# A state-space layer and a mixer MLP on one core: the spectrum of the second chunk taken once, kernel sums a step sooner, part of x loaded by GpSimd

## The chip, the core and the metric

The kernel runs on one core of a Trainium2 chip, as one program. The core has TensorE (PE, with its weight loads as PEld), VectorE (DVE), ScalarE (ACT), GpSimd (POOL) and SyncE (SP), which issues most of the transfers between device memory and the core's own memory. The metric is device time of one execution in microseconds (us), as the median of several runs. One execution was also recorded by the hardware profiler; all rows below come from it.

## The reference

```python
def reference(u, log_A_real, A_imag, C_real, C_imag, log_dt, D_skip, w1, b1, w2, b2, c, w_mod):
    sa, ca, ga, sb, cb, gb = split(silu(c) @ w_mod, 6)        # each [448]
    h = layernorm(u) * (1 + ca) + sa                          # u: [2048, 448]
    # S4D: kernel K[d, l] = 2 Re sum_n C[d,n] exp(A[d,n] dt[d] l), 256 modes, 2048 taps
    y = irfft(rfft(h.T, 4096) * rfft(K, 4096))[:, :2048].T + h * D_skip
    x = u + ga * y
    h = layernorm(x) * (1 + cb) + sb
    # token-mixing MLP over the 2048 rows, 1792 hidden units, shared by the 448 columns
    h = layernorm(h)
    return x + gb * (gelu(h.T @ w1 + b1) @ w2 + b2).T
```

## The kernel before

**Steps.** The taps of K come from exponentials and sines, made in 56 steps of 8 columns (`NHALF`). A step is written as: `st_phase` (TensorE, L608: phases `xe`, `xg` from `lph` and `tab`, for the step after), `st_step` (ScalarE: six activations L649 to L654 on the phases; VectorE: the four products `E`; GpSimd: the two products `G`), and `st_kgen` (TensorE, L683: 32 small products of `G` and `E` into `kg`; after each second step ScalarE copies `kg` to `ks`, L697). `st_kgen` of step s stood in the code of step s + 2. The steps go in seven batches of 8; each opens with a `window`, in which ScalarE takes the 16 exponentials (L619) of the batch and TensorE the exponents, and in which the last two `st_kgen` of the batch before stand. `st_s1` (L721) transforms finished taps into `yk`.

**The Fourier product in pieces.** The columns of K are handled in two chunks of 224; a chunk has 16 pieces. For a piece n:

- `pc_load` (SyncE): `u`, a part of the spectrum of h that was written to memory as `us_d` earlier (L744 in the second chunk, L747 in the first), and tables `si` (L750, L752);
- `pc_s2` (TensorE, L780): `kx`, the spectrum of K, a table times `yk`;
- `pc_mul` (VectorE, L788): two products `z` of `kx` and `u`;
- `pc_inv` (TensorE, L796 and L797): `vv`, the inverse of the two `z`;
- `pc_out` (ScalarE, L802, then SyncE): copy to `vt` and write to `v_d`.

An fp32 matmul makes two records in the profile. The first chunk's pieces are put between the steps from step 33 on by `piece`: on odd steps a new piece's `pc_s2`, on even ones its `pc_inv`. The second chunk runs alone after the steps, in a loop over k (L1133), with loads three pieces ahead. Its order on TensorE is kx of the next piece, then vv of this one. In the second chunk `kx` was made twice, once by a table with the real part in both halves of the partitions and once by that table with its halves exchanged and a sign (`pc_swap` for the first piece, `pc_tables` for the others, tile `sw`, L761, L768, L769). GpSimd made the third table of a piece from the second (L770, L771). Each of the two was multiplied by the same `u`.

**Start.** x has 2048 rows, held as 16 rows `r` for each of 128 partitions (`xt`). Rows 0 to 3 are loaded by GpSimd, rows 4 to 15 by SyncE (`x_load`, L299, four transfers a call), ahead of the loads that the steps ask for: `lph` and `lex` (L594, L598: parameters) and blocks of w_mod (L324, `wm`, 784 KB each, by the table `late`: blocks 2 and 3 in steps 2 and 3). `u_stats` (L499) takes the statistics of rows 2s and 2s + 1 in step s, on VectorE in the middle of `st_step`. `modulation` (L486) multiplies a block of w_mod with the condition; block 2 is first asked for at the end of step 4.

**Order.** TensorE, ScalarE, VectorE and GpSimd run in the order in which the code is written. SyncE does so up to step 8 and near the end of the second chunk, and in between a scheduler sets its order. Every engine works its queue in order: whatever stands behind a waiting instruction waits too. After the second chunk the layer norms and the two MLP products follow (L1181 to L1183, L1304 to L1306).

Of the kernel before, what the change touches and what calls it, by code (L numbers as in the profile page):

```python
# [11 lines left out]
F32 = mybir.dt.float32  # L12
# [10 lines left out]
P = 128  # L23
# [16 lines left out]
def dft_tables():  # L40
    n1 = np.arange(32)
    k1 = np.arange(32)
    n2 = np.arange(64)
    k2 = np.arange(64)
    nn = 4096
    t = {}
    w = 2 * np.pi * np.outer(n1, k1) / 64
    w1 = np.zeros((2, 32, 32))
    w1[0] = np.cos(w)
    w1[1] = -np.sin(w)  # L50
    w1[0, :, 0] = 1
# [12 lines left out]
    def inverse(rows, cols, k, m, ang):  # L64
        a = np.cos(ang) * 2 / nn
        b = np.sin(ang) * 2 / nn
        i1[0, rows, k, m[0]] = a
        i1[1, rows, k, m[0]] = -b
        i2[1, rows, k, m[0]] = -a
        i2[0, rows, k, m[0]] = -b  # L70
        if len(m) > 1:
            i1[0, rows, k, m[1]] = b
            i1[1, rows, k, m[1]] = a
            i2[1, rows, k, m[1]] = -b
            i2[0, rows, k, m[1]] = a

    for k in range(1, 32):
        ang = 2 * np.pi * np.outer(n2, k + 64 * k2) / nn
        s[0, :, k, 0] = np.cos(ang)
        s[1, :, k, 0] = np.sin(ang)  # L80
        s[0, :, k, 1] = -np.sin(ang)
        s[1, :, k, 1] = np.cos(ang)
        inverse(slice(None), None, k, (0, 1), ang.T)


    for q in range(32):
        ang = 2 * np.pi * n2 * (32 + 64 * q) / nn
        s[1, :, 0, 0, q] = np.cos(ang)
        s[1, :, 0, 1, q] = -np.sin(ang)
        inverse(q, None, 0, (1,), ang)  # L90
    for q in range(33, 64):
        ang = 2 * np.pi * n2 * (64 * (q - 32)) / nn
        s[0, :, 0, 0, q] = np.cos(ang)
        s[0, :, 0, 1, q] = -np.sin(ang)
        inverse(q, None, 0, (0,), ang)
    s[0, :, 0, 0, 32] = 1
    s[0, :, 0, 1, 32] = (-1.0) ** n2
    i1[0, 32, 0, 0] = 1 / nn
    i2[1, 32, 0, 0] = (-1.0) ** n2 / nn
    s2 = s.reshape(P, 32 * P)  # L100

    t["S2"] = s.reshape(2, 4, 8, 2, 32 * P).transpose(3, 0, 2, 1, 4).reshape(P, 32 * P)

    one = np.einsum("cnk,cqkm->km", w1, s.reshape(2, 64, 32, P))
    t["SV"] = one[ones_k1()].T

    order = lambda a: a.reshape(P, 32, 2, 2, 2, 16).swapaxes(3, 4)
    t["I1"] = order(i1)
    t["I2"] = order(i2)
    ft = np.zeros((32, 2, 2, 32, 2))  # L110
    w = 2 * np.pi * np.outer(k1, n1) / 64
    f0 = np.cos(w)
    f1 = -np.sin(w)
    f0[0] = 1
    f1[0] = (-1.0) ** n1
    for h in range(2):
        ft[:, 0, h, :, h] = f0
        ft[:, 1, h, :, h] = f1
    t["FT"] = ft.reshape(P, 64)


    te = np.zeros((3, 64, 16, 32))
    tg = np.zeros((3, 16, 4, 16, 32))
    n = np.arange(32)
    for d in range(16):
        te[0, 2 * d : 2 * d + 2, d] = 2 * n + 1
        te[2, 2 * d : 2 * d + 2, d] = -n
        tg[0, d, 0:2, d] = n
        tg[0, d, 2:4, d] = 1
        tg[2, d, 0:2, d] = -64 * n  # L130
        tg[2, d, 2:4, d] = 1
    tg = tg.reshape(3, 16, 2, 2, 512).swapaxes(1, 2)
    tt = np.concatenate([te.reshape(3, 64, 512), tg.reshape(3, 64, 512)], 1)
    tt[1] = -tt[0]
    t["TT"] = tt.reshape(3, P, 512)

    v1, v2 = (t.pop(k).reshape(2, 64, 32, P) for k in ("I1", "I2"))
    j1 = np.stack([v1[0], v2[1]])  # L140
    j2 = np.stack([v1[1], v2[0]])
    for nm, tabs, n in (("SI", (s2, v1, v2), NP), ("SJ", (s2, j1, j2), 1)):
        t[nm] = np.stack([a.reshape(P, NP, 2, P)[:, :n] for a in tabs], 2).reshape(P, n * 6 * P)

    re = np.stack([s[:, :, :, 0]] * 2, 3)
    t["SK"] = np.stack([a.reshape(P, NP, 2, P) for a in (re, v1)], 2).reshape(P, NP * 4 * P)
    return {k: np.ascontiguousarray(v.astype(np.float32)) for k, v in t.items()}


# [72 lines left out]
def tile_adaln_s4d_mixer(ctx, tc, i, out):  # L224
# [20 lines left out]
    with ExitStack() as es:  # L245
# [49 lines left out]

        def x_load(r0, n, eng=nc.sync):
            for g in range(4):
                rr = slice(r0, r0 + n)
                eng.dma_start(xt[32 * g : 32 * g + 32, rr], xv[rr, g].rearrange("r n d -> n r d"))  # L299


        mg = cg.tile([P, 2, P], BF16, name="mg")
# [301 lines left out]
        def halves(out, lhs, rhs, start, stop):  # L604

            for k in range(2):
                r = slice(64 * k, 64 * k + 64)
                T.matmul(out[k], lhs[r], rhs[r], start=start, stop=stop)  # L608
# [147 lines left out]

        def pc_swap(n):

            pw[n] = swp.tile([P, 2, P], F32, tag="sw", name="sw")
            halves = lambda t: t.rearrange("p j (h m) -> p j h m", h=2)  # L760
            S.copy(halves(pw[n]), halves(pl[n][1][:, 0])[:, :, ::-1])  # L761

        def pc_tables(n):


            re, to, back = (pl[n][1][:, t] for t in range(3))
            pw[n] = im = swp.tile([P, 2, P], F32, tag="sw", name="sw")
            S.activation(im[0:64], re[64:128], AF.Copy, scale=-1.0)  # L768
            S.copy(im[64:128], re[0:64])  # L769
            G.tensor_copy(back[0:64], to[64:128])  # L770
            G.tensor_scalar(back[64:128], to[0:64], -1.0, None, ALU.mult)  # L771

        def pc_s2(n):
            c, p = divmod(n, NP)
            k1 = yks[c][:, 2 * p : 2 * p + 2]
            pk[n] = [(pxs if c else pms).tile([P, 2, DC], F32, tag="ms", name="kx") for _ in range(c + 1)]
            tabs = [pl[n][1][:, 0]] + ([pw.pop(n)] if c else [])
            for j in range(2):
                for kx, t in zip(pk[n], tabs):
                    T.matmul(kx[:, j], t[:, j], k1[:, j], start=True, stop=True)  # L780

        def pc_mul(n):
            c, p = divmod(n, NP)
            u = pl[n][0]
            pz[n] = []
            for cc in range(2):
                z = fp.tile([P, 2, DC], F32, tag=f"z{cc}", name=f"z{cc}")
                V.tensor_tensor(z, pk[n][cc if c else 0], u[:, 0 if c else cc], ALU.mult)  # L788
                pz[n].append(z)
            pk.pop(n)  # L790

# [124 lines left out]
        for g in (1, 2):  # L916
            load(g, False)
        wm_load(1, wm_slot(1))
        x_load(4, 4)
        x_load(8, 8)  # L920
        remainder()

        def chains():
# [43 lines left out]
        def window(s):  # L967
# [12 lines left out]
            for e in range(BATCH):  # L980
# [15 lines left out]
                if s == 8 and e == 1:  # L996

                    tt(mod[0], mod[0], mod[2], ALU.mult)
                if e < 2 and s:
                    st_kgen(s - 2 + e)  # L1000
                elif e == 5:
                    if s == 8:
                        yks[0] = y0.tile([P, 32, DC], F32, tag="yk", name="yk0")
                    st_s1(s > 16)
# [28 lines left out]
        for s in range(tail):  # L1033
# [30 lines left out]
            if s >= NHALF:  # L1064
                flush(dve)
                mellow()
            else:
                if s % BATCH > 1:
                    st_kgen(s - 2)
                if (s + 1) % BATCH:  # L1070
                    st_phase(s + 1)
                elif s + 1 < NHALF:
                    st_exponents(s + 1)
                st_step(s, between)
            flush(act)
            if s == NHALF:
                st_kgen(s - 2)
                st_kgen(s - 1)

            free = s > 7 and not st_s1(s % BATCH == BATCH - 1)  # L1080
            if s + 2 < 32 and (s + 2) % BATCH > 1:
                st_mag2(s + 2)
# [50 lines left out]
        for k in range(NP + 1):  # L1133

            n = NP + k
            if k < NP:
                if n + 3 < 2 * NP:
                    pc_load(n + 3)
                pc_s2(n)
                pc_mul(n)  # L1140
            if k + 1 < NP:
                pc_tables(n + 1)
            if k:
                pc_inv(n - 1)
                pc_out(n - 1)
            if k == NP - 4:
                last = ExitStack()
                last.enter_context(tc.manual_schedule(engines={ENG.SP}))

            if k in (NP - 3, NP - 2):  # L1150
                wst.load()
                if k == NP - 3:
                    x_pair(0)
# [184 lines left out]
```

## Time and profile before

| what | us |
|---|---|
| median of 3 runs | 752.48 |
| their lowest and highest | 751.7, 760.46 |
| the profiled execution: its time | 759.6 |
| its span, first to last instruction | 757.8 |

| stretch of the profiled execution | us from the span's start |
|---|---|
| steps 0 to 31 | 27 to 253 |
| steps 32 to 55, with the first chunk's pieces | 253 to 386 |
| second chunk | 399 to 449 |
| layer norms and MLP | 449 to 758 |

A row of a timeline is: start, duration, engine, line, operation, out<-in with shapes and count, and in brackets the idle time of the engine just before it and what ended it. A row of groups is: line, engine, operation, names, shapes and count, then busy us in total, mean ns of one, and idle time before with its releasers. A row of windows is: stretch, its length, busy us of PE, PEld, DVE, ACT and POOL with counts, granted TensorE clock (1.00 is full), DMA share (mean busy share of the 16 DMA engines) and GB/s.

### The profile page before, as it was taken

How to read it: one execution, taken by the hardware profiler on the slowest of the kernel's cores; microseconds unless marked ns; L12 is line 12 of the kernel's file. 1: busy time of each engine (PE TensorE's matmuls, PEld its weight loads, DVE VectorE, ACT ScalarE, POOL GpSimd, SP SyncE). 2: the span in 40 equal slices, each digit the busy share in tenths (PEclk: the TensorE clock that was granted, in tenths of full speed). 3: DMA queues.
4: the chain of work that ended last, by engine and by line, in shares of the span. 5: the costliest groups of instructions: out<-in, count | busy, mean ns of one | idle time of the engine just before them, and what ended most of it. 6: DMA issues, size and time to landing. Idle time of an engine off the chain costs nothing. (4 is left out here: it accounts for less than half of the span.)

```text
span 757.8 us, 18128 instructions
## 1 busy us (share of the span) xinstructions
PE 667.6 (88%) x7136; PEld 497.6 (66%) x7136; DVE 453.4 (60%) x875; ACT 448.3 (59%) x842; POOL 249.4 (33%) x289
## 2 busy tenths in 40 slices
PE   1779989969789878888889966999999999999997
PEld 0435334535435556556579963777899999999996
DVE  7695878599478568584863335677752253433341
ACT  5956587788687788988944445777742242222220
POOL 6573456438337766766733310000000000000000
PEclk9878657969899889999999995999999999999999
DMA  6884545286777736545456789985566426566540
GB/s 166 235 175 116 172 142 176 74 251 172 206 188 240 201 87 166 141 129 151 114 161 205 238 229 264 224 217 160 141 190 207 144 68 189 154 173 181 148 134 25
DMA packets 97106, 127.99 MB, mean 169 GB/s; under 512 B 12922, under 2 KB 78206, under 8 KB 96894
## 3 DMA queue, kind: packets, MB, share of 16 engines
q1 hardware_dynamic: 96398, 125.14, 59.4%
q0 software_dynamic: 624, 1.70, 0.8%
q8 instruction: 56, 0.92, 0.5%
q14 instruction: 28, 0.23, 0.1%
HBM read 91.46 MB, written 34.87 MB: 167 GB/s over the span
## 5 line engine op out<-in xcount | busy, mean ns | idle before, releaser
L209 ACT CAST whi<-w 128x896 fp32r<-128x896 f32 x64 | 59.8, 939 | 131.4 <-PE o L1305 84.7
L656 POOL TENSOR_TENSOR G<-mag,gs 128x512 f32<-128x512 f32 x56 | 71.8, 1282 | 119.0 <-ACT gs L652 118.9
L218 DVE TENSOR_TENSOR wlo<-w,whi 128x896 fp32r<-128x896 f32 x64 | 67.9, 1086 | 40.3 <-ACT whi L209 27.9
L1181 PE MATMUL acc<-h3h,whi 128*128 128x448 f32 x224 | 83.6, 373 | 0.0
L1182 PE MATMUL acc<-h3l,whi 128*128 128x448 f32 x224 | 82.2, 367 | 0.0
L608 PE MATMUL xg<-tab,lph 64*128 64x512 f32 x112 | 68.6, 615 | 15.1 <-ACT xg L654 8.4
L683 PEld LDWEIGHTS kg<-E,G 128*32 128x32 f32 x3584 | 61.2, 122 | 31.0 <-issue 15.9
L1183 PE MATMUL acc<-h3h,wlo 128*128 128x448 f32 x224 | 81.4, 364 | 0.0
L1305 PE MATMUL o<-ul,whi 128*128 128x448 f32 x224 | 81.3, 363 | 0.0
L1304 PE MATMUL o<-uh,whi 128*128 128x448 f32 x224 | 81.2, 362 | 0.0
L1306 PE MATMUL o<-uh,wlo 128*128 128x448 f32 x224 | 80.6, 360 | 0.0
L608 PE MATMUL xe<-tab,lph 64*128 64x512 f32 x112 | 66.6, 602 | 11.1 <-ACT gs L653 9.3
L683 PE MATMUL kg<-E,G 128*32 128x64 f32 x3584 | 71.4, 239 | 5.3 <-issue 4.9
L657 POOL TENSOR_TENSOR G<-mag,gs 128x512 f32<-128x512 f32 x56 | 71.9, 1284 | 0.0
L658 DVE TENSOR_TENSOR E<-m,xe 128x512 f32<-128x512 f32 x56 | 38.1, 681 | 49.2 <-ACT xe L651 23.6
L637 POOL TENSOR_TENSOR m<-mag,w 128x512 f32<-128x512 f32 x56 | 59.8, 1068 | 5.6 <-DVE E L662 1.2
L788 DVE TENSOR_TENSOR z<-kx,u 128x448 f32<-128x448 f32 x64 | 36.8, 616 | 41.1 <-PE kx L780 41.1
L1308 DVE SCALAR_TENSOR_TENSOR y<-o,b,mod 128x448 f32<-128x448 f32 x16 | 10.9, 684 | 80.3 <-PE o L1306 80.3
L649 ACT ACTIVATE ab<-xe 128x512 f32<-128x512 f32 x56 | 33.5, 599 | 33.0 <-PE xe L608 18.7
L1181 PEld LDWEIGHTS acc<-h3h,whi 128*128 128x128 f32 x224 | 42.7, 191 | 13.0 <-ACT h L1236 7.8
L608 PE MATMUL xe<-tab,lex 64*128 64x512 f32 x56 | 31.8, 584 | 16.5 <-DMA lex<-wm 15.9
L619 ACT ACTIVATE mag<-xe 128x512 f32<-128x512 f32 x56 | 34.2, 611 | 18.9 <-PE xg L608 10.6
(222 smaller groups left out, 1545.2 us busy)
## 6 DMA issues: line engine op xcount, KB each, us to landing
w<-in_B_w_dram SPq DMA_DIRECT2D x64, 224.0 KB
w<-in_B_w_dram SPq DMA_DIRECT2D x32, 448.0 KB
u<-us_d SPq DMA_DIRECT2D x48, 224.0 KB
yu_d<-yt SPq DMA_DIRECT2D x16, 448.0 KB
yi<-yu_d SPq DMA_DIRECT2D x16, 448.0 KB
us_d<-uo SPq DMA_DIRECT2D x16, 448.0 KB
v_d<-vt SPq DMA_DIRECT2D x32, 224.0 KB
vt<-v_d SPq DMA_DIRECT2D x16, 448.0 KB
```

What stands on the lines that cost most here:

```text
L209: self.nc.scalar.copy(hi, w)
L218: eng.tensor_tensor(lo, w, hi.bitcast(F32), ALU.subtract)
L608: T.matmul(out[k], lhs[r], rhs[r], start=start, stop=stop)
L656: G.tensor_tensor(Gt[:, 1], mg_, v32(sg), ALU.mult)
L657: G.tensor_tensor(Gt[:, 0], mg_, v32(cg_), ALU.mult)
L683: T.matmul(kgs[g][32 * q : 32 * q + 32, m], Gt[:, c, d], E[:, c, d], start=h == 0 and c == 0 and m == 0, stop=h == 1 and c == 1, skip_grou ...
L1181: nc.tensor.matmul(acc[f], hi[:, fs], h3h[:, r], start=r == 0, stop=False)
L1182: nc.tensor.matmul(acc[f], hi[:, fs], h3l[:, r], start=False, stop=False)
L1183: nc.tensor.matmul(acc[f], lo[:, fs], h3h[:, r], start=False, stop=r == 15)
L1304: nc.tensor.matmul(o, hi[:, ks], uh[kh][:, k], start=kh == 0 and k == 0, stop=False)
L1305: nc.tensor.matmul(o, hi[:, ks], ul[kh][:, k], start=False, stop=False)
L1306: nc.tensor.matmul(o, lo[:, ks], uh[kh][:, k], start=False, stop=kh == 1 and k == 6)
```

## The change

Three edits.

1. In the second chunk `kx` is made once, by the table `s2` that the first chunk has too (real part in one half of the partitions, imaginary part in the other). The first `z` is `kx` times `u`, the second `kx` times `u` with its halves exchanged. `pc_swap` now copies `u` (two copies of 64 partitions by 448 columns, by ScalarE) for every piece, a piece ahead, and `pc_tables` has three GpSimd instructions where it had two, and none on ScalarE. The memory table `SK` holds `s2` and `v1`, as large as before.
2. From step 33 on, `st_kgen` of step s stands in the code of step s + 1, behind the phase.
3. Rows 4 to 7 of x are loaded by GpSimd behind its work of step 0, rows 8 to 15 behind that of step 1, in transfers of the same sizes.

```diff
+    for nm, tabs, n in (("SI", (s2, v1, v2), NP), ("SJ", (s2, j1, j2), 1), ("SK", (s2, v1), NP)):
...
         def pc_swap(n):
-            pw[n] = swp.tile([P, 2, P], F32, tag="sw", name="sw")
-            halves = lambda t: t.rearrange("p j (h m) -> p j h m", h=2)
-            S.copy(halves(pw[n]), halves(pl[n][1][:, 0])[:, :, ::-1])
+            pw[n] = swp.tile([P, 2, DC], F32, tag="sw", name="sw")
+            for h in range(2):
+                S.copy(pw[n][64 * h : 64 * h + 64], pl[n][0][64 - 64 * h : 128 - 64 * h, 0])
 
         def pc_tables(n):
-            re, to, back = (pl[n][1][:, t] for t in range(3))
-            pw[n] = im = swp.tile([P, 2, P], F32, tag="sw", name="sw")
-            S.activation(im[0:64], re[64:128], AF.Copy, scale=-1.0)
-            S.copy(im[64:128], re[0:64])
-            G.tensor_copy(back[0:64], to[64:128])
-            G.tensor_scalar(back[64:128], to[0:64], -1.0, None, ALU.mult)
+            like, unlike = pl[n][1][:, 1], pl[n][1][:, 2]
+            G.tensor_copy(unlike[0:64], like[64:128])
+            G.tensor_copy(unlike[64:128], like[64:128])
+            G.tensor_scalar(like[64:128], like[0:64], -1.0, None, ALU.mult)
 
         def pc_s2(n):
-            pk[n] = [(pxs if c else pms).tile([P, 2, DC], F32, tag="ms", name="kx") for _ in range(c + 1)]
-            tabs = [pl[n][1][:, 0]] + ([pw.pop(n)] if c else [])
+            pk[n] = (pxs if c else pms).tile([P, 2, DC], F32, tag="ms", name="kx")
             for j in range(2):
-                for kx, t in zip(pk[n], tabs):
-                    T.matmul(kx[:, j], t[:, j], k1[:, j], start=True, stop=True)
+                T.matmul(pk[n][:, j], pl[n][1][:, 0, j], k1[:, j], start=True, stop=True)
 
         def pc_mul(n):
-                V.tensor_tensor(z, pk[n][cc if c else 0], u[:, 0 if c else cc], ALU.mult)
+                V.tensor_tensor(z, pk[n], pw.pop(n) if c and cc else u[:, cc], ALU.mult)
...
         first_chain()
-        x_load(4, 4)
-        x_load(8, 8)
...
         def window(s):
-                if e < 2 and s:
-                    st_kgen(s - 2 + e)
+                if s and e < (2 if s <= 32 else 1):
+                    st_kgen(s - (2 if s <= 32 else 1) + e)
...
-                if s % BATCH > 1:
+                if s < 32 and s % BATCH > 1:
                     st_kgen(s - 2)
                 if (s + 1) % BATCH:
                     st_phase(s + 1)
                 elif s + 1 < NHALF:
                     st_exponents(s + 1)
+                if s > 32 and s % BATCH:
+                    st_kgen(s - 1)
                 st_step(s, between)
             flush(act)
             if s == NHALF:
-                st_kgen(s - 2)
                 st_kgen(s - 1)
+            if s < 2:
+                x_load(4 + 4 * s, 4 + 4 * s, G)
...
             if k + 1 < NP:
                 pc_tables(n + 1)
+                pc_swap(n + 1)
```

Line numbers of the changed kernel are lower by 4 to 8 from the tables on (L683 is L679 there, L780 is L772, L796 and L797 are L788 and L789, L299 is L295).

**TensorE, steps 36 and 37.** The end of the phase of one step, a sum `kg`, the inverse `vv` of a piece and the beginning of the next phase. Before:

```order
L608 MATMUL xe<-tab,lph_142 128x512
L608 MATMUL xg<-tab,lph_142 128x512
L796 MATMUL vv<-z_3982,si 128x224
L797 MATMUL vv<-z_3984,si 128x224
L796 MATMUL vv<-z_3982,si 128x224
L797 MATMUL vv<-z_3984,si 128x224
L683 MATMUL kg<-E,G 32x64 x32
L608 MATMUL xe<-tab,lph_143 128x512
L608 MATMUL xg<-tab,lph_143 128x512
```

And in the changed kernel:

```order
L604 MATMUL xe<-tab,lph_142 128x512
L604 MATMUL xg<-tab,lph_142 128x512
L679 MATMUL kg<-E,G 32x64 x32
L788 MATMUL vv<-z_4014,si 128x224
L789 MATMUL vv<-z_4016,si 128x224
L788 MATMUL vv<-z_4014,si 128x224
L789 MATMUL vv<-z_4016,si 128x224
L604 MATMUL xe<-tab,lph_143 128x512
L604 MATMUL xg<-tab,lph_143 128x512
```

The sum has moved from behind vv to ahead of it, and it is that of a step later.

**ScalarE, beginning of the second chunk.** `yk` is the last transform of the taps, `sw` the swapped tile, `vt` the copy out. Before:

```order
L727 COPY yk_3487<-y_5856 128x32x2x8
L802 COPY vt<-vv 128x448
L761 COPY sw<-si 128x256
L768 ACTIVATE sw<-si 64x256
L769 COPY sw<-si 64x256
L768 ACTIVATE sw<-si 64x256
L769 COPY sw<-si 64x256
L802 COPY vt<-vv 128x448
```

And in the changed kernel:

```order
L723 COPY yk_3487<-y_5856 128x32x2x8
L794 COPY vt<-vv 128x448
L757 COPY sw<-u 64x448 x6
L794 COPY vt<-vv 128x448
L757 COPY sw<-u 64x448 x2
L794 COPY vt<-vv 128x448
```

Two copies of `u` a piece stand where two of the table stood, still ahead of the vt of two pieces earlier.

**SyncE and GpSimd, steps 0 to 4.** `wm_79` is w_mod, `lph` the parameters, `pars` their place in memory. SyncE before:

```order
L324 DMA wm_79<-in_w_mod_dram 112x4x448
L299 DMA xt<-in_A_u_dram 32x1792 x4
L299 DMA xt<-in_A_u_dram 32x3584 x4
L594 DMA lph_142<-pars_57 32x256
L598 DMA lph_142<-pars_57 64x1x256
L324 DMA wm_79<-in_w_mod_dram 112x4x448 x2
```

GpSimd in the changed kernel, from the products of step 0 on:

```order
L652 TENSOR_TENSOR G<-mag,gs 128x512
L653 TENSOR_TENSOR G<-mag,gs 128x512
L295 DMA xt<-in_A_u_dram 32x1792 x4
L631 TENSOR_TENSOR w<-mag 128x16
L633 TENSOR_TENSOR m_417<-mag,w 128x512
L652 TENSOR_TENSOR G<-mag,gs 128x512
L653 TENSOR_TENSOR G<-mag,gs 128x512
L295 DMA xt<-in_A_u_dram 32x3584 x4
```

The two L299 rows have left SyncE's queue, so that `lph_142` and the blocks of w_mod follow the first block directly, and stand in GpSimd's between the products of a step and the tables `m` of a later one.

More of the change, by code (lines that the diff above doesn't have):

```diff
@@ L141, in dft_tables @@
     j2 = np.stack([v1[1], v2[0]])
[L142 to L148, printed above, removed]
+    for nm, tabs, n in (("SI", (s2, v1, v2), NP), ("SJ", (s2, j1, j2), 1), ("SK", (s2, v1), NP)):
+        tabs = [a.reshape(P, NP, 2, P)[:, :n] for a in tabs]
+        t[nm] = np.stack(tabs, 2).reshape(P, n * len(tabs) * 2 * P)
     return {k: np.ascontiguousarray(v.astype(np.float32)) for k, v in t.items()}
@@ L297, in x_load @@
             for g in range(4):
-                rr = slice(r0, r0 + n)
-                eng.dma_start(xt[32 * g : 32 * g + 32, rr], xv[rr, g].rearrange("r n d -> n r d"))
+                to = xt[32 * g : 32 * g + 32, r0 : r0 + n].rearrange("n r d -> n (r d)")
+                eng.dma_start(to, x.rearrange("(n g r) d -> g n (r d)", g=4, r=16)[g, :, r0 * D : (r0 + n) * D])
         mg = cg.tile([P, 2, P], BF16, name="mg")
```

## Prediction

> **What bounds the kernel now.** I read the page first: shares, clock, and the chain that ended last.
>
> ```profile
> span 757.8 us, 18128 instructions
> PE 667.6 (88%) x7136; PEld 497.6 (66%) x7136; DVE 453.4 (60%) x875; ACT 448.3 (59%) x842; POOL 249.4 (33%) x289
> ...
> PEclk9878657969899889999999995999999999999999
> ...
> PE acc L1181 6%; PE acc L1182 6%; PE o L1305 6%; PE acc L1183 6%; PE o L1304 6%; PE o L1306 6%; PE kx L780 3%; PE y L1209 2%; PE vv L796 1%; PE vv L797 1%; DMA w<-in_B_w_dram 1%; DMA v_d<-vt 1%; SPq L1189 0%; SPq L1127 0%; ACT vt L802 0%
> ```
>
> TensorE leads; its granted clock is full (9) in the slices from 303 to 454 us. But half of this chain is the MLP (L1181 to L1306), which the change doesn't touch. What it touches is three stretches, each with a bound of its own, and no two of them overlap. So I price each and add.
>
> The second chunk (401 to 448 us) is TensorE alone. The chain in order of time shows it piece after piece:
>
> ```profile
> 425.87 1.51 PE kx L780 x8
> 427.38 0.38 PE vv L796 x2
> ...
> 428.52 0.38 PE vv L797 x2
> 428.89 1.51 PE kx L780 x8
> ```
>
> A piece takes 428.89 - 425.87 = 3.02 us, eight kx records and eight vv records of 0.189 us (1.51 / 8) with no wait between them.
>
> The kernel loop (steps 33 to 55) is a ring. Here is one pair of steps from the timeline, all engines, with the idle time and its releaser in brackets:
>
> ```profile
> 371.12 0.60 ACT L649 ACTIVATE ab<-xe 128x512 f32<-128x512 f32 x1 [0.76 <-PE xe L608]
> 374.25 0.60 ACT L649 ACTIVATE ab<-xe 128x512 f32<-128x512 f32 x1
> 374.50 1.14 DVE L788 TENSOR_TENSOR z<-kx,u 128x448 f32<-128x448 f32 x2
> 374.52 1.27 POOL L657 TENSOR_TENSOR G<-mag,gs 128x512 f32<-128x512 f32 x1
> 375.17 0.65 PE L796 MATMUL vv<-z,si 128*128 128x224 f32 x2 [1.06 <-DVE z L788]
> 377.03 1.10 PE L683 MATMUL kg<-E,G 128*32 128x64 f32 x64
> 377.25 0.55 ACT L802 COPY vt<-vv 128x448 f32<-128x448 f32 x1
> 378.06 0.50 PE L608 MATMUL xe<-tab,lph 64*128 64x512 f32 x1
> 378.20 0.37 ACT L697 COPY ks<-kg 128x256 f32<-128x256 f32 x1 [0.40 <-PE kg L683]
> 379.33 0.60 ACT L649 ACTIVATE ab<-xe 128x512 f32<-128x512 f32 x1 [0.76 <-PE xg L608]
> ```
>
> A pair lasts 379.33 - 371.12 = 8.21 us. ScalarE has two steps of 374.25 - 371.12 = 3.13 us, a vt copy and a ks copy in it, and stands idle for 0.40 + 0.76 us: it waits for kgen (377.03), and then for the phase (378.06) behind kgen. TensorE had itself been idle 1.06 us in front of vv.
>
> The start (28 to 62 us) waits for transfers. Rows of SyncE, VectorE, TensorE and GpSimd:
>
> ```profile
> 28.52 9.85 SPq L299 DMA_DIRECT2D xt<-in_A_u_dram  x8
> 40.95 1.27 SPq L324 DMA_DIRECT2D wm<-in_w_mod_dram  x2
> 41.91 0.63 DVE L499 BATCH_NORM_STATS2 st<-xt 128x6 f32<-128x448 f32 x1 [1.58 <-DMA xt<-in_A_u_dram]
> 57.24 3.35 PE L486 MATMUL pm<-wm,scb 112*128 112x448 f32 x4 [4.63 <-DMA wm<-in_w_mod_dram]
> ```
>
> Eight transfers of x hold SyncE's queue until 38.4, then come two blocks of w_mod, and TensorE stands from 52.61 to 57.24 for the first of them.
>
> **Part A, the spectrum once.** Each of the 16 pieces of the second chunk loses four of its eight kx records: 4 x 0.189 = 0.76 us, 16 x 0.76 = 12.1 us, if TensorE stays the bound. The first kx also loses a wait for the swapped table:
>
> ```profile
> 400.25 0.65 PE L780 MATMUL kx<-yk,sw 128*128 128x224 f32 x2 [0.59 <-ACT sw L761]
> ```
>
> That is 0.6 us. A piece is then 3.02 - 0.76 = 2.27 us. What is late next?
>
> ```profile
> L802 ACT COPY vt<-vv 128x448 f32<-128x448 f32 x32 | 17.3, 539 | 32.4 <-PE vv L797 19.8 <-issue 9.9 <-DMA v_d<-vt 1.8
> L788 DVE TENSOR_TENSOR z<-kx,u 128x448 f32<-128x448 f32 x64 | 36.8, 616 | 41.1 <-PE kx L780 41.1
> L769 ACT COPY sw<-si 64x256 f32<-64x256 f32 x15 | 6.0, 403 | 0.2
> L770 POOL COPY si<-si 64x256 f32<-64x256 f32 x15 | 5.9, 395 | 35.8 <-DMA si<-in_SK_dram 19.7 <-issue 8.0 <-PE vv L797 7.2
> L771 POOL TENSOR_SCALAR si<-si 64x256 f32<-64x256 f32 x15 | 12.7, 847 | 1.0
> ```
>
> ScalarE now swaps u in two copies of 64x448. Nothing of that shape stands in the trace: at least 0.40 each (L769, fewer columns), at most the 0.54 of L802 (same columns, from PSUM). I take 0.54, the same column count: 2 x 0.54 + 0.54 for vt = 1.6 us. VectorE stays at 2 x 0.62 = 1.2. GpSimd makes 0.40 + 0.40 + 0.85 = 1.65. All lie under 2.27, beside TensorE. ScalarE's swap of piece n+1 stands ahead of vt of n-1 and needs u a piece earlier than before. What lies queued behind it is vt, then the write of v_d, then SyncE's next u. The landing is judged from these rows:
>
> ```profile
> 438.04 0.33 SPq L752 DMA_DIRECT2D si<-in_SK_dram  x1
> 441.20 0.39 POOL L770 COPY si<-si 64x256 f32<-64x256 f32 x1 [1.01 <-DMA si<-in_SK_dram]
> ```
>
> Table 31 was in use 441.20 - 438.04 = 3.2 us after its issue. It is issued at the end of vv 27 and wanted by kx 31 two pieces later, 4.5 us at the new pace, so the buffers still reach. The traffic may not:
>
> ```profile
> 415.00:420.00 5.00, 5.00 (x28) 5.00 (x27) 2.25 (x4) 2.27 (x6) 2.48 (x4) 1.00 0.85 281
> 425.00:430.00 5.00, 5.00 (x28) 5.00 (x27) 1.32 (x3) 2.34 (x6) 1.68 (x4) 1.00 0.76 218
> ```
>
> The last two columns are DMA share and GB/s. A piece moves u, table and v_d, 224 + 256 + 224 KB = 0.721 MB. At full share these rows give 281 / 0.85 = 331 or 218 / 0.76 = 287 GB/s, so 2.18 to 2.51 us for a piece, on both sides of 2.27. I take the middle, 2.35, which costs 16 x 0.08 = 1.3 us. **A: 12.1 + 0.6 - 1.3 = 11.4 saved**; with 2.51 it is 8.9, with transfers that can't go faster than now it is 0.6, with no limit 12.7.
>
> **Part B, the sums a step sooner.** TensorE's order in a pair changes from vv, kgen, phase to kgen, vv, phase. The kgen (1.03 us, 377.03 to 378.06) goes into the 1.06 us in which TensorE waited for z. The phase then follows vv directly, about 377.0 to 378.2 with its L608 matmuls as long as before (378.06 to 379.33), and ScalarE has until 371.12 + 2 x 3.13 + 0.55 + 0.37 = 378.3 of its own work. So the pair becomes about 7.2 us, and its two waits, 1.16 us, all but go. Such brackets on ScalarE run from the row at 291.15 to that at 379.33:
>
> ```profile
> 291.15 0.60 ACT L649 ACTIVATE ab<-xe 128x512 f32<-128x512 f32 x1 [0.76 <-PE xe L608]
> ```
>
> Three pairs have both waits (1.16 or 1.17), two have 0.76 alone, two 0.41 alone: 5.8 us in all. In each of the two later windows of exponentials two kgens stood between the first exponents and now one does:
>
> ```profile
> 303.24 0.60 ACT L619 ACTIVATE mag<-xe 128x512 f32<-128x512 f32 x1 [1.06 <-PE xg L608]
> 347.60 0.60 ACT L619 ACTIVATE mag<-xe 128x512 f32<-128x512 f32 x1 [1.55 <-PE xg L608]
> 388.32 1.83 PEld L683 LDWEIGHTS kg<-E,G 128*32 128x32 f32 x128 [0.28 <-issue]
> ```
>
> One kgen less is 1.0 us in each, within both waits; and behind the last step (388.32) two kgens in a row become one, 1.0 more. Together 5.8 + 2.0 + 1.0 = 8.8. TensorE itself needs 8.21 - 1.06 = 7.15 us of a pair, so it is as full as ScalarE and small slips will show: **B: 8 saved**, between 3 and 9. The wait added is kgen for G of the step before. G of the step of 371.12 ended at 375.79 (374.52 + 1.27); its kgen is now asked for at 378.2. It is covered by 2.4 us. Queued behind a kgen that waited would be vv or kx and the next phase, and ScalarE behind that.
>
> **Part C, rows of x by GpSimd.** SyncE is free at 28.5 instead of 38.4 and issues the two blocks of w_mod some 10 us sooner, behind one reload of lph. GpSimd issues eight transfers instead:
>
> ```profile
> 7.66 2.00 POOL L299 DMA_DIRECT2D xt<-in_A_u_dram  x4
> 43.19 1.27 POOL L656 TENSOR_TENSOR G<-mag,gs 128x512 f32<-128x512 f32 x1 [1.46 <-ACT gs L652]
> 40.00:45.00 5.00, 5.00 (x28) 1.97 (x28) 3.35 (x7) 3.09 (x6) 3.46 (x5) 0.50 0.95 202
> ```
>
> Its own four took 0.5 us each; SyncE's took 9.85 / 8 = 1.23. I take 0.5, the same engine: 2 us behind step 0's G and 2 behind step 1's. G of step 2 slips by about 4 us and step 3 finds GpSimd late; from 43.19 on it had 1.46 us spare and VectorE, busy until 47.1 with what stands ahead of E of step 3, covers the rest. At 1.23 it would be 6 us more on GpSimd and about 3 beyond that cover. The engines were full (share 0.95 at 202 GB/s). Before TensorE's question at 52.61, there are two blocks of w_mod and twelve rows of x to move from 28.0 on: 2 x 0.80 + 2.75 = 4.35 MB, 21.5 us at 202 GB/s, done at 49.5. So the wait of 4.63 should go whole. Rows 4 to 7 were waited for until 41.91. They are now issued at 32 to 34 and share the engines with w_mod: at best they land by 40.3 (1.6 gained), at worst last of all at 49.5 (7.6 lost on VectorE). I take no change, with 0.6 off for slips. **C: 4 saved**, between 6 saved and 4 lost.
>
> [...]
>
> **The sum.** 11.4 + 8 + 4 = 23.4 us. The profiled execution took 759.6 us (span 757.8 and 1.8 around it), which gives 736.2. It lies 7.1 above the median of the runs, 752.48 (751.7 to 760.46). Nearly all of A and B comes from slices at the full clock, so their sizes should hold in a quicker execution: 752.5 - 23.4 = 729.1, and I say **730**.
>
> **Rivals.**
> 1. Transfers set the second chunk. For it: share 0.76 to 0.85 already, and GpSimd waits 19.7 us for tables (L770). Against: share 0.85 came with 281 GB/s, not with a stall of TensorE. At 2.7 us a piece A is 16 x 0.32 + 0.6 = 5.7; total 752.5 - 17.7 = 734.8, or 740 with A at 0.6.
> 2. C's wait is exchanged for another, x landing late for VectorE or w_mod for TensorE. For: the full engines. C at 0: 733; at 4 lost: 737.
> 3. B yields little, since ScalarE (7.2) and TensorE (7.15) are both full and pass the wait round. Against: the 1.06 us hole is as long as kgen. B at 2: 735.
> 4. Slower: kgen waits for G. It is one place: TensorE's queue behind the phase in steps 33 to 55, with kx, vv and the next phase behind it. Each us that G ends after the phase costs a us in some 22 steps. With B gone, the gain of A and C (15.4) is used up at 15.4 / 22 = 0.7 us of wait, and 1.0 us gives 752.5 - 15.4 + 22 = 759. It needs G 3.1 us later than in the rows above. GpSimd makes 2 x 1.28 us in a step of 3.5, nothing is added to it there, so I hardly believe it.
> 5. The change does not do what it says: the same number of kx, or sums not sooner. The order of instructions shows both moved, so this has no weight of its own.
>
> **Chances.** Forecast with all three (724 to 736): 0.62. Rival 1 (734 to 741): 0.15. Rival 2 (732 to 738): 0.10. Rival 3 (734 to 738): 0.09. Rival 4 (752 to 765): 0.04. Two per cent, about what a measurement of this kernel can tell from no change, is 737.4 at the lower side and 767.5 at the upper. Below 737.4 lie nearly all of the forecast and some half of rivals 1 to 3: 0.62 + 0.17 = 0.78; as executions here spread over 9 us I say 0.75, within 0.22, slower 0.03. The range reaches from 722 (everything at its best, 12.7 + 9 + 6 = 27.7, and a quick execution) to 745 (two rivals together, or a median from the upper runs).
>
> **What would show it.** Right: kx in the second chunk with 64 records fewer and a piece at 2.3 to 2.4 us; no row of L486 waiting 4 us for wm in step 4; ScalarE's step pairs at 7.2 us with no ks wait and no bracket before the step's first row. Wrong in A: brackets on kx or sw with a DMA as releaser. Wrong in B: kg rows released by GpSimd, or pairs still above 7.8. Wrong in C: L499 waiting longer for xt, or G late for ScalarE (L650). What would upset it all is a clock at 0.50 in the second chunk, where every TensorE term doubles.

## The result, and the profile after

The changed kernel took **735.36 us** in the median (733.2 to 741.83, 4 runs), the kernel before beside it 752.12 us; the ratio is 0.9747, with a 95% interval from 0.9703 to 0.9792, which is 19 us of 752. (The ratio leaves disturbed runs out, so it lies a little lower than the quotient of the medians.) A second set gave 736.50 us and 0.9762 (0.9711 to 0.9813). The forecast was 730, with a range from 722 to 745.

The page of the changed kernel: span, engines, clock by slice, and the lines of the chain that ended last.

```profile
span 731.6 us, 17983 instructions
PE 640.9 (88%) x7072; PEld 478.8 (65%) x7072; DVE 449.5 (61%) x869; ACT 453.9 (62%) x849; POOL 258.6 (35%) x312
PEclk9869779989799989999999958999999999999999
PE acc L1177 7%; PE o L1300 6%; PE acc L1179 6%; PE acc L1178 6%; PE o L1302 6%; PE o L1301 6%; DMA si<-in_SK_dram 2%; PE y L1205 2%; PE vv L789 1%; PE vv L788 1%; DMA w<-in_B_w_dram 1%; PE kx L772 1%; DMA v_d<-vt 1%; SPq L1185 0%; SPq L1122 0%
```

TensorE has 7072 matmuls, 64 fewer. In the chain kx fell from 3% to 1%, and a transfer that was not there before, the table `si`, now has 2%.

**Second chunk.** TensorE's rows in the timeline, four columns of time and name, idle time in brackets:

```profile
388.94 0.92 PE L772 MATMUL kx<-yk,si 128*128 128x224 f32 x4
389.69 0.54 PE L788 MATMUL vv<-z,si 128*128 128x224 f32 x2
...
391.21 0.92 PE L772 MATMUL kx<-yk,si 128*128 128x224 f32 x4
391.96 0.54 PE L788 MATMUL vv<-z,si 128*128 128x224 f32 x2
...
394.29 1.02 PE L772 MATMUL kx<-yk,si 128*128 128x224 f32 x4 [0.65 <-DMA si<-in_SK_dram]
```

A piece without a wait takes 391.21 - 388.94 = 2.27 us, as worked out. The next takes 3.08, since its table was not there. That table's issue, on SyncE:

```profile
389.18 0.33 SPq L748 DMA_DIRECT2D si<-in_SK_dram  x1
```

From here to 394.29 it took 5.1 us; the later tables that an engine waited for took 3.7 to 4.5. The forecast had 3.2, which is the last table of the chunk before. Others of that chunk already took longer, this one 4.4 us from its issue to GpSimd's first use:

```profile
431.99 0.33 SPq L752 DMA_DIRECT2D si<-in_SK_dram  x1
436.41 0.39 POOL L770 COPY si<-si 64x256 f32<-64x256 f32 x1 [2.76 <-DMA si<-in_SK_dram]
```

**Start of the MLP.** TensorE's first product there, before and after:

```profile
456.42 1.76 PE L1209 MATMUL y<-vt,ft 128*64 128x448 f32 x4 [7.86 <-DMA vt<-v_d]
```

```profile
430.87 1.76 PE L1205 MATMUL y<-vt,ft 128*64 128x448 f32 x4 [9.40 <-DMA vt<-v_d]
```

The wait for v is 1.5 us longer: part of what the chunk won is given back.

**Kernel loop.** ScalarE's rows, steps 43 to 45 of the changed kernel:

```profile
311.69 0.37 ACT L693 COPY ks<-kg 128x256 f32<-128x256 f32 x1 [1.76 <-PE kg L679]
311.95 0.60 ACT L645 ACTIVATE ab<-xe 128x512 f32<-128x512 f32 x1
...
315.37 0.63 ACT L645 ACTIVATE ab<-xe 128x512 f32<-128x512 f32 x1
...
319.02 0.37 ACT L693 COPY ks<-kg 128x256 f32<-128x256 f32 x1 [0.52 <-PE kg L679]
319.28 0.60 ACT L645 ACTIVATE ab<-xe 128x512 f32<-128x512 f32 x1
```

The pair takes 319.28 - 311.95 = 7.33 us instead of 8.21. The wait for the phase is gone; 0.52 us for kgen is left, and at 311.69 a new wait of 1.76 stands.

**Start.** GpSimd's eight issues (4 in each row), VectorE's first row of rows 4 to 7, its last read of `xg` for the step before, and TensorE's next phase:

```profile
32.22 2.00 POOL L295 DMA_DIRECT2D xt<-in_A_u_dram  x4
38.06 2.00 POOL L295 DMA_DIRECT2D xt<-in_A_u_dram  x4
45.86 0.63 DVE L495 BATCH_NORM_STATS2 st<-xt 128x6 f32<-128x448 f32 x1 [5.98 <-DMA xt<-in_A_u_dram]
48.72 0.67 DVE L658 TENSOR_TENSOR E<-m,xg 128x512 f32<-128x512 f32 x1
49.50 0.76 PE L604 MATMUL xg<-tab,lph 64*128 64x512 f32 x1 [6.37 <-issue]
```

An issue by GpSimd took 0.5 us here (2.00 / 4). The wait for w_mod is gone, but rows 4 to 7 came at 45.86 instead of 41.91; VectorE stood for 5.98 us, and step 4 behind it: the profile names no releaser for TensorE's 6.37 us ("issue"), but the phase begins 0.1 us after VectorE's L658 ends at 49.39. Even so step 6 starts at 61.3 instead of 64.0.

By stages (starts of steps from ScalarE's first row of each, L645, L649 before; the chunk from the first vv of piece 16 to the last vv; then to the first acc of the MLP; us):

| profile | step 8 at | steps 32 to 55 | 55 to chunk | chunk | to first acc |
|---|---|---|---|---|---|
| before | 99.5 | 116.6 | 20.5 | 45.2 | 20.1 |
| changed | 95.1 | 113.2 | 16.4 | 36.7 | 21.6 |
| changed, second set | 96.9 | 110.4 | 17.2 | 37.4 | 21.5 |
| A alone | 99.4 | 116.3 | 18.3 | 36.7 | 21.5 |
| B alone | 99.3 | 115.2 | 18.6 | 45.2 | 20.2 |
| C alone | 96.8 | 116.5 | 20.6 | 45.2 | 19.9 |

The two profiled executions lie 26 us apart. Of that, 6.7 us are in steps 8 to 32, which the change doesn't touch: 166.4 us before, 159.7 after, and anything from 159.6 to 166.1 in the twelve profiles below. That is how executions differ, not the change.

### The profile page after: what moved, and what is told of

The parts are those of the page before. It is cut to its first block, busy times and chain, and to the rows that moved or that the text cites. A ratio compares the mean times of both kernels' runs of the same rounds, so it can differ in the third digit from the quotient of the medians.

```text
span 731.6 us, 17983 instructions
## 1 busy us (share of the span) xinstructions
PE 640.9 (88%) x7072; PEld 478.8 (65%) x7072; DVE 449.5 (61%) x869; ACT 453.9 (62%) x849; POOL 258.6 (35%) x312
## 5 line engine op out<-in xcount | busy, mean ns | idle before, releaser
L604 PE MATMUL xg<-tab,lph 64*128 64x512 f32 x112 | 65.2, 584 | 20.9 <-ACT xg L650 8.9
L679 PEld LDWEIGHTS kg<-E,G 128*32 128x32 f32 x3584 | 57.3, 116 | 31.7 <-issue 18.1
L604 PE MATMUL xe<-tab,lph 64*128 64x512 f32 x112 | 63.5, 573 | 13.1 <-ACT gs L649 7.4
L679 PE MATMUL kg<-E,G 128*32 128x64 f32 x3584 | 66.9, 230 | 3.9 <-issue 3.4
L645 ACT ACTIVATE ab<-xe 128x512 f32<-128x512 f32 x56 | 33.9, 606 | 23.4 <-PE xe L604 13.4
L780 DVE TENSOR_TENSOR z<-kx,u 128x448 f32<-128x448 f32 x48 | 28.4, 619 | 31.2 <-PE kx L772 31.1
L615 ACT ACTIVATE mag<-xe 128x512 f32<-128x512 f32 x56 | 34.6, 618 | 17.1 <-PE xg L604 12.8
```

The source lines that it names most:

```text
L679: T.matmul(kgs[g][32 * q : 32 * q + 32, m], Gt[:, c, d], E[:, c, d], start=h == 0 and c == 0 and m == 0, stop=h == 1 and c == 1, skip_grou ...
```

## The experiments

### Each part alone

A_alone is the kernel before with part A alone; in short (the tables of SK as in the change):

```
+ S.copy(pw[n][64*h : 64*h+64], pl[n][0][64-64*h : 128-64*h, 0])   # u swapped
- for kx, t in zip(pk[n], tabs): T.matmul(kx[:, j], t[:, j], ...)
+ T.matmul(pk[n][:, j], pl[n][1][:, 0, j], ...)
...
```

> The kernel before with part A alone (the spectrum once, u swapped by ScalarE). Theory 1 (a piece is TensorE's but for transfers that run at their limit): vv to vv 2.4 to 2.5 us on average instead of 3.02, second chunk 8.5 us shorter over 15 pieces, 1.4 more at its first piece, about 1 us of it lost at the start of the MLP: 8 to 10 us saved, 742 to 744. Rival (transfers alone set it, and the rest of the change makes them overlap): piece at 2.7, 5 to 6 saved, 746 to 747.

Measured: 747.15 us (743.36 to 750.04), ratio 0.9895 (0.985 to 0.9941): 7.9 us, between 4.5 and 11.3. The stages say 2.2 + 8.5 - 1.4 = 9.3. The chunk is 36.7 us alone as well as with the rest (36.7 and 37.4), so the parts hardly disturb each other there.

B_alone is the kernel before with the sums a step sooner:

```
- if s % BATCH > 1: st_kgen(s - 2)        # ahead of the phase; windows and end as in the change
+ if s < 32 and s % BATCH > 1: st_kgen(s - 2)
+ if s > 32 and s % BATCH: st_kgen(s - 1) # behind the phase
```

> The kernel before with part B alone (sums a step sooner from step 33 on). Theory 1 (the pair becomes TensorE's own 7.3 us and ScalarE's wait for the phase turns into one for kgen): steps 32 to 55 some 3.5 us shorter, 2 us more between step 55 and the second chunk: 5 to 6 saved, 746 to 747. Rival (B is worth the 8 us of the forecast, and a stretch of half clock that fell into steps 32 to 43 hid the rest in the profile of the change): pairs at 7.3 and 8 saved, 744.

Measured: 748.54 us (743.88 to 751.96), 0.9923 (0.989 to 0.9955): 5.8 us, between 3.4 and 8.3. Its profile shows only 1.4 us in steps 32 to 55 and 1.9 behind them. Why it differs from the second set of the changed kernel, which shows 6.2 in the same steps, is read from the clock. Two stretches of 3.4 us in steps 40 to 42, first of the second set and then of the changed kernel; columns are the stretch, its length, busy time of PE, PEld, DVE, ACT and POOL (with instructions), granted clock, DMA share, GB/s:

```profile
302.00:305.40 3.40, 2.10 (x11) 1.43 (x8) 1.25 (x2) 3.37 (x6) 2.06 (x4) 1.00 0.44 117
305.40:308.80 3.40, 2.29 (x60) 1.49 (x64) 2.69 (x6) 3.37 (x8) 2.77 (x3) 1.00 0.45 137
```

```profile
301.00:304.40 3.40, 1.37 (x6) 0.74 (x4) 2.29 (x4) 3.36 (x8) 2.14 (x3) 1.00 0.55 149
304.40:307.80 3.40, 3.02 (x47) 1.98 (x51) 2.85 (x5) 3.40 (x9) 2.77 (x3) 0.56 0.18 60
```

In the first steps behind a window of exponentials TensorE is idle for 1.1 to 2.0 us of 3.4. In the changed kernel's profile 3.4 us at half clock follow, and then the wait of 1.76 us at 311.69; in the second set there is no such stretch, and the same wait reads:

```profile
312.39 0.37 ACT L693 COPY ks<-kg 128x256 f32<-128x256 f32 x1 [0.26 <-PE kg L679]
```

Now the whole loop, one row each: before, A alone, the second set of the changed kernel, the changed kernel, B alone.

```profile
265.90:382.50 116.60, 98.22 (x1965) 67.86 (x1963) 78.19 (x135) 103.25 (x199) 78.89 (x80) 0.97 0.50 132
```

```profile
264.90:381.20 116.30, 99.96 (x1965) 68.38 (x1963) 78.48 (x135) 103.14 (x198) 78.68 (x80) 0.94 0.52 136
```

```profile
258.30:368.70 110.40, 100.95 (x2052) 70.54 (x2054) 79.37 (x134) 103.43 (x203) 79.58 (x81) 0.97 0.54 142
```

```profile
254.90:368.10 113.20, 103.78 (x2056) 72.56 (x2059) 79.34 (x133) 103.47 (x204) 78.55 (x81) 0.95 0.52 137
```

```profile
261.20:376.50 115.30, 104.95 (x2056) 74.00 (x2059) 79.01 (x133) 103.70 (x204) 79.22 (x81) 0.93 0.53 137
```

With the old order the loop takes 116.3 to 116.6 us at a mean clock of 0.97 as at 0.94: TensorE had a hole in each pair (1.06 us before vv at 375.17), and half clock filled it: its busy time grew from 98.22 to 99.96 us and the loop didn't. With the new order it takes 110.4 at 0.97, 113.2 at 0.95 and 115.3 at 0.93: the hole is used up, and TensorE's slow stretches come through. ScalarE's waits say the same. Between the second set and the changed kernel two of them differ, 0.26 against 1.76 us (above) and, behind the window of step 32, 2.23 against 3.47; that is 2.7 of the 2.8 us between the loops.

Profiles with either order, by the time at half clock (worked back from the means in stretches of 3.4 us):

| order | half clock in the loop, us | length of the loop, us |
|---|---|---|
| old: before, C alone, A alone | 6.8, 10.2, 13.6 | 116.6, 116.5, 116.3 |
| new, four profiles (second set, I, G, J) | 6.8 | 110.4 to 111.5 |
| new: the changed kernel | 10.2 | 113.2 |
| new: B alone | 17.1 | 115.3 |

So at 6.8 us of half clock B is worth 5.1 to 6.2 us in the loop. Behind it lie 1.9 more (1.1 in the second set): 7.0 to 7.7 us profile by profile. This is read across executions that differed by themselves; no run set the clock on purpose.

TensorE was not idle in the stretch ahead of the half clock: it was busy for 1.37 us of 3.4 (301.00 to 304.40). In the second set it was busy for 2.10 us of the stretch from 302.00, and full clock followed.

C_alone is the kernel before with rows 4 to 15 of x by GpSimd:

```
- x_load(4, 4); x_load(8, 8)                      # SyncE, ahead of w_mod
+ if s < 2: x_load(4 + 4 * s, 4 + 4 * s, G)       # behind steps 0 and 1
```

> The kernel before with part C alone (rows 4 to 15 of x by GpSimd). Theory 1: rows 4 to 7 land about 4 us later (VectorE's first wait for xt ends near 45.9 instead of 41.9), TensorE's wait for w_mod in step 4 is gone, step 8 starts 4 us sooner, and that stays: 748. Rival (the lead at step 8 is given back further on, or lies in the execution that was profiled): 751 to 753, no change.

Measured: 751.84 us (746.51 to 758.06), 0.9953 (0.9921 to 0.9985): 3.5 us, between 1.1 and 6.0. Step 8 starts at 96.8 instead of 99.5, and rows 4 to 7 come at 46.6. In the seven profiles with this start step 8 lies between 95.1 and 96.9, in the three with the old one between 99.3 and 99.5, so the gain of 2.4 to 4.4 us there is clear.

E_changed_again is the changed kernel itself, in a second set of runs.

> The changed kernel once more, so that its time stands beside the next three from the same runs. The three parts alone saved 7.9, 5.8 and 3.5 us; if they add up and nothing is traded between them, 17 us under the kernel before of this set (ratio 0.977). If part A's shorter chunk and part B's fuller TensorE get in each other's way, 0.983 or more.

Measured: 736.5 us (731.96 to 737.6), 0.9762 (0.9711 to 0.9813). The three parts alone add to 17.2 us, the change saved 19.0 and 18.0 in its two sets: they add up within the intervals.

### What holds the pair at 7.33

D_copy_late and H_copy_half put the ks copy behind the next step's activations, D each time and H for the first of each two sums.

```
- act.append(copy)
+ (held if s > 32 and (s + 1) % BATCH else act).append(copy)   # D; H adds "and not o"
+ act.extend(held); held.clear()                               # at each step's start
```

> The changed kernel, with ScalarE's copy of a finished sum (ks) put behind the next step's six activations instead of ahead of them, from step 33 on. Theory 1 (TensorE's own work sets the pair): the bracket on ks of 0.52 to 0.69 us goes but comes back as a wait for the phase; pairs stay at 7.3 to 7.5, time within 1.5 us of the changed kernel (734 to 737). Rival (the ring through ks on ScalarE sets it): pairs at ScalarE's own 7.18 or a little under, some 3 to 4 us less: 731 to 732.

> The changed kernel, with the ks copy behind the next step's six activations only for the first of each two sums, so that the y products keep their place (in D_copy_late they moved into the windows, which waited 3.7 and 6.1 us). Theory 1 (the ring through ks makes the pair 7.33, as the pairs of 7.17 in D_copy_late say, and D lost its time in the windows alone): pairs alternate between 7.17 and 7.33 or 7.5, windows without a wait, 0.5 to 1 us less than the changed kernel. Rival (a copy put late costs on its own): some 5 us more, as half of D.

Measured: D 747.06 us, 0.9913 (0.988 to 0.9946); H 741.0 us, 0.9815 (0.974 to 0.9891). ScalarE's step starts in D:

```profile
272.10 0.60 ACT L645 ACTIVATE ab<-xe 128x512 f32<-128x512 f32 x1 [1.09 <-PE xg L604]
...
279.27 0.60 ACT L645 ACTIVATE ab<-xe 128x512 f32<-128x512 f32 x1 [0.23 <-PE xg L604]
...
286.44 0.60 ACT L645 ACTIVATE ab<-xe 128x512 f32<-128x512 f32 x1 [0.23 <-PE xg L604]
```

A pair is 7.17 us, of which ScalarE works 6.94 and waits 0.23 for the phase. TensorE does the same work in it, so the 7.33 was not TensorE's sum, as my first theory had it, but the ring through ks: phase, kgen, ks copy, next step. D is slower than the changed kernel all the same; for H the medians say so too, but the intervals overlap. In D the y products move into the windows, where ScalarE then waits 3.67 and 6.12 us (rows at 296.32 and 343.86). In H pairs of 8.4 and 6.6 us alternate (steps at 270.9, 279.3 and 285.9; the loop took 114.0 us at a mean clock of 0.92), and behind step 55 it needs 18.5 us where the changed kernel needs 16.4 and 17.2. So my expectation for H fell: H did not win the 0.16 us of a pair. By that mean its loop had some 18 us of half clock (2 x 0.08 x 114.0), about as much as B alone's, so how much of its length is the copy's place stays open, and so does what made the pairs uneven. In both D and H the weight loads of kgen now wait for GpSimd's G, 0.55 us at 275.99 in D and at 274.76 in H, where 0.35 with no such releaser is usual in the changed kernel.

### What holds the pieces of the second chunk

F_half_u leaves out every second load of u (the piece multiplies with the u of the piece before); I_table_lead gives the tables from piece 20 on six buffers of their own and issues them a piece sooner.

```
# F
+ if n > NP and n % 2: u = pl[n - 1][0]
# I
+ tables[n] = w = pool.tile([P, 3, 2, P], F32, tag="st", name="si")   # bufs=6
+ if n + 4 < 2 * NP: table_load(n + 4, sip)
```

> The changed kernel; in the second chunk every second piece multiplies with the u of the piece before, so half of the u loads (8 x 224 KB, a sixth of the traffic of a piece) are left out. Theory 1 (in the second chunk and behind it the transfers are what is late): no wait of kx for a table, vv to vv 2.27 to 2.32 us instead of 2.45 on average (2 us), and the MLP's first wait for vt back from 9.4 towards 7.9 us: 3 to 4 us less than the changed kernel. Rival (the 0.18 us come from ScalarE, which swaps u and copies vt in order, and from the landing time of single transfers): still 2.4 to 2.45, within 1 us of the changed kernel.

> The changed kernel; in the second chunk the tables from piece 20 on go to six buffers of their own and are asked for a piece sooner, with no wait for an old buffer (same bytes). Theory 1 (TensorE's waits there are the landing time of a table, some 5 us, against a lead of two pieces, 4.5 us; half of the u loads left out changed nothing): no wait of kx for a table, 15 pieces in 34.1 to 35.0 us instead of 36.6 to 37.4, 1.5 to 2.5 us less than the changed kernel, unless the MLP's first wait for vt grows by as much. Rival (the engines' throughput sets the pieces after all): tables land later in turn, 36.5 us again, no change. Beside it, in steps 32 to 55: if TensorE without slack now pays for half-clock stretches, their length there is some 107 us and 0.45 us for each us of half clock.

Measured: F 736.38 us, 0.9755 (0.9683 to 0.9828), chunk 36.6 us. Its engines over 10 us, against the changed kernel's:

```profile
410.00:420.00 10.00, 9.74 (x52) 9.26 (x51) 4.93 (x9) 6.98 (x13) 6.51 (x12) 1.00 0.78 236
```

```profile
405.00:415.00 10.00, 9.95 (x53) 9.45 (x52) 5.21 (x10) 7.45 (x14) 7.01 (x14) 1.00 0.99 317
```

The share fell from 0.99 to 0.78. In F's timeline TensorE waits for a table all the same:

```profile
402.17 1.02 PE L777 MATMUL kx<-yk,si 128*128 128x224 f32 x4 [0.35 <-DMA si<-in_SK_dram]
```

In I no kx waits for a table; what is left is the first piece, whose z waits for the swapped u:

```profile
387.67 0.62 DVE L790 TENSOR_TENSOR z<-kx,sw 128x448 f32<-128x448 f32 x1 [0.39 <-ACT sw L767]
...
396.40 0.92 PE L782 MATMUL kx<-yk,si 128*128 128x224 f32 x4
...
398.67 0.92 PE L782 MATMUL kx<-yk,si 128*128 128x224 f32 x4
```

The chunk takes 35.4 us, 1.3 to 2.0 less than in the two profiles of the changed kernel, and every piece but the first 2.27. So the landing time of a table (up to 5.1 us) against the lead of two pieces (4.5 us) made the waits, not the throughput. The time doesn't show it: 736.37 us, 0.978 (0.9725 to 0.9836); 1 to 2 us are under what these runs resolve. Steps 32 to 55 took 110.8 us in I with 6.8 us of half clock; 107 + 0.45 x 6.8 = 110 was expected.

### The start, and versions that might be faster

G_x_early lets GpSimd issue rows 4 to 7 in its idle stretch ahead of step 0's G (run in two sets); J_both is G with I; K_mlp_loads_early is J with the MLP's first loads two pieces earlier.

```
# G
+ S.activation(one, one, AF.Sin); x_load(4, 4, G)      # end of window 0
+ if s == 1: x_load(8, 8, G)
# K
- if k in (NP - 3, NP - 2): wst.load()
+ if k in (NP - 5, NP - 4): wst.load()
```

> The changed kernel, with GpSimd's four transfers of rows 4 to 7 ahead of its first product of step 0 (issued near 22 us, in its idle stretch) instead of behind it (32 us). Theory 1 (VectorE's wait of 5.98 us for rows 4 to 7 is order, not traffic): L495 finds its rows, step 4 starts near 46 to 47 instead of 51.2, and some 3 us of that are left at step 8: 3 us less than the changed kernel. Rival (the engines are full from 30 to 50 us, so what rows 4 to 7 win is lost by w_mod, lph or rows 8 to 15): step 8 at 95 to 97 as before, no change.

> The changed kernel with G_x_early's early rows and I_table_lead's tables. Theory: the two lie 300 us apart and add up, 2 to 3 us from the start and 1 to 2 from the second chunk: ratio to the kernel before 0.967 or less (G_x_early alone 0.970). Rival: the second chunk gives its gain back at the MLP's first wait for vt: 0.970.

> J_both, with the two first weight blocks of the MLP and the first pair of x rows issued two pieces earlier in the second chunk (same bytes). The stretch from the chunk's last vv to the MLP's first product is 21.2 to 21.7 us in the profiles that have part A with ks in its place, and 19.9 to 20.2 in those without A. Theory 1 (what stands in front of the MLP's first load of v is the backlog of these 1.3 MB, since the shorter chunk gives them less time): first wait for vt down from 9.5 to 8 us or less, the stretch near 20 us, 1.5 us less than J_both. Rival (the writes of v and their reading back set it, whatever was issued before): 21.5 us again, no change, or tables late in the last pieces (kx waiting) that cost as much.

> G_x_early once more, beside K_mlp_early's runs, to settle whether it beats the changed kernel (ratios to the kernel before: 0.9747 and 0.9762 for the changed kernel, 0.9696 for G_x_early and 0.9747 for J_both, each within half a per cent). Theory (2 to 3 us are won at the start and kept): 0.971 to 0.973. Rival (the 0.9696 was a set of executions with little half clock): 0.975 to 0.977. In its profile: step 8 at 93.5 to 94.5 by both.

Measured: G 731.34 us, 0.9696 (0.9641 to 0.975), and again 735.18 us, 0.9704 (0.9656 to 0.9753); J 733.14 us, 0.9747 (0.9701 to 0.9793); K 733.79 us, 0.9704 (0.9654 to 0.9753). The waits in G, VectorE's and TensorE's:

```profile
53.84 0.63 DVE L495 BATCH_NORM_STATS2 st<-xt 128x6 f32<-128x448 f32 x1 [2.01 <-DMA xt<-in_A_u_dram]
54.23 3.35 PE L482 MATMUL pm<-wm,scb 112*128 112x448 f32 x4 [2.13 <-DMA wm<-in_w_mod_dram]
```

The wait of 5.98 us for rows 4 to 7 is gone, and w_mod (2.1 us; 4.8 in the second profile) and the later rows are late instead. Step 8 starts at 93.7, 95.0, 94.3 and 94.5 in the four profiles with early rows, and at 95.1 to 96.9 in the seven with the changed kernel's start: about 2 us on average, where I expected 3. G's two ratios lie half a per cent below the changed kernel's two, but their intervals overlap and J's doesn't show it. That G beats the changed kernel is likely and not settled.

K's first wait of the MLP, and what it cost in the last piece of the chunk, on ScalarE and TensorE:

```profile
PE y L1219 <- DMA vt<-v_d: 7.3, 1, 7.3
```

```profile
423.88 1.14 ACT L767 COPY sw<-u 64x448 f32<-64x448 f32 x2 [5.15 <-DMA u<-us_d]
424.70 0.62 PE L798 MATMUL vv<-z,si 128*128 128x224 f32 x2 [2.03 <-DVE z L790]
```

The wait for v fell from 9.5 to 7.3 us (8.4 to 10.2 in all other profiles with part A) and the stretch to the first acc from 21.7 to 19.7: the backlog of weights is what delays v, as the theory had it. But u now stands behind that backlog, and the chunk took 38.3 instead of 35.4. Chunk and stretch together are 58.0 in K and 57.1 in J: the bytes issued earlier made others late.

## Why the prediction was right, point by point

The time came out 5 us above the forecast, within its range, and faster with it. The mechanisms were those of the text; the sizes were too large.

- **A, 11.4 forecast, about 9 found** (7.9 by the times). The piece of 2.27 and the lost wait ahead of the first kx were right. Two terms were mis-sized. The transfers' 1.3 were 2.1 to 2.7: 1.4 to 2.0 for late tables and 0.7 for the first swapped u, which the sum didn't have. The step that failed is "3.2 us, wanted 4.5 us later, so the buffers still reach": the 3.2 was the last table of a chunk with less traffic, where others took up to 4.5, and in the faster chunk they took 3.7 to 5.1. The throughput bound beside it (2.18 to 2.51 us) gave nearly the right price for the wrong reason, as F and I show. And 1.5 us are given back at the MLP's first wait for v, which no term held. Rival 1 names the place but not the mechanism.
- **B, 8 forecast, 5.8 by the times.** At the least half clock seen the profiles give 7.0 to 7.7. The failed step is the sentence that A and B lie in slices at full clock, so that their sizes hold in any execution. Closing TensorE's hole made the loop pay for each half-clock stretch, and B is worth anything from 3.3 (B alone's own profile: 1.4 + 1.9) to 7.7. The pairs came to 7.33, not 7.2, since ScalarE still waits 0.52 for kgen; the windows lost both of their waits, as the text had it, and behind step 55 it was 1.9 rather than 1.0. The fear that kgen would wait for G (rival 4) did not come true in the changed kernel: the new waits are for kgen itself. But the margin is smaller than the 2.4 us of the text, 1.2 us at the kgen of 317.85 (its G ended at 316.64), and in D and H it is gone.
- **C, 4 forecast, 3.5 by the times.** 0.5 us for an issue and w_mod's wait were right. The landing of rows 4 to 7 was not: four to five us later, not unchanged, inside the bound of 49.5 that the text gave. That the total came so near is in part luck. Rival 2, the full engines (share 0.95 at 202 GB/s), would have made C zero. The rows show that what was won for one transfer was lost by another (G and K show it twice), but the times put C at 1.1 to 6.0, above zero: which transfer was late mattered.
- **The sum.** The base of 752.5 was right; 23.4 became 17 to 19.

## What to carry to other kernels

A hole in an engine's queue isn't only waste. Here TensorE's 1.06 us a pair absorbed its slow stretches: with the hole the loop took 116.3 to 116.6 us at 6.8 to 13.6 us of half clock, without it 110.4 to 115.3 at 6.8 to 17.1. When an edit closes it, price the edit at the worst clock seen in the traces as well as at full clock. And when a loop gets faster, take the landing time of its prefetches from the fullest traffic in the trace (here up to 5.1 us, where the last table of the slower chunk had 3.2), and compare it with the lead at the new pace.

## What was unexpected of the hardware

The half-clock stretches of the loop came in steps of 3.4 us: 6.8 us from 260.4 and 3.4 from 304.8 in the changed kernel, 6.8 from 271.4 in the one before. The changed kernel's loop again, after window 32:

```profile
258.00:261.40 3.40, 1.09 (x6) 0.68 (x7) 2.85 (x5) 3.37 (x8) 2.50 (x2) 0.86 0.20 61
261.40:264.80 3.40, 3.40 (x71) 2.31 (x69) 2.83 (x5) 3.36 (x8) 2.63 (x3) 0.50 0.15 47
264.80:268.20 3.40, 3.40 (x32) 1.95 (x36) 2.35 (x5) 0.82 (x2) 2.39 (x2) 0.64 0.03 9
```

Worked back from the means, the clock was half for 0.28 x 3.4 + 3.4 + 0.72 x 3.4 = 6.8 us here, and for 3.4 us at 304.4 (0.88 + 0.12 of 3.4, with the next stretch at 0.94). TensorE was full while it lasted (3.40 of 3.40 us in the row at 0.50) and busy for less than half of the time before it (1.09 and 1.37 of 3.40 in the rows from 258.00 and 301.00). Cut where the clock changes, the stretch at 304.4 and the one before it read:

```profile
301.40:304.80 3.40, 0.99 (x6) 0.39 (x5) 2.57 (x4) 3.37 (x7) 2.37 (x2) 1.00 0.56 156
304.80:308.20 3.40, 3.40 (x63) 2.33 (x67) 2.57 (x4) 3.40 (x8) 2.64 (x3) 0.50 0.19 67
```

In the profiles of the changed kernel and of the one before, from 250 us to the end of the steps, one grid of stretches 3.413 us long can be laid for each (through 260.433 in the first and 271.423 in the second) so that all 74 stretches read 0.50 or 1.00. Of those at full clock, four were followed by one at half clock: TensorE was busy in them for 0.47 and 1.00 us in the changed kernel (from 257.02 and 301.39), and for 0.47 and 2.51 in the one before (from 268.01 and 250.94). Of those followed by full clock the least busy had 2.10 us (from 345.77) and 1.99 (from 312.38). So three of the four came behind the three least busy stretches, and the fourth doesn't fit an order by busy time. That the pauses cause the half clock is read from this order; no run changed them on purpose. Why the second set's loop got no half clock behind the window of step 40 isn't shown beyond its busy time of 2.10 us. I had read the clock as a matter of the slice; by these rows it went, three times in four, with what TensorE did in the 3.4 us before.
